# A new table of places and engines for the first recurrence of an attention and MLP kernel

## The chip, the cores and the metric

The kernel runs on one core of a Trainium2 chip. Its time is the device time of one execution in microseconds. A core has a matrix engine (PE, with its weight loads PEld), and the engines DVE, ACT and POOL that work on vectors; SP issues transfers. Matrix results land in PSUM, eight banks of 128 partitions by 512 fp32 numbers, from where DVE or ACT copies them out (an "eviction").

## The reference

The kernel computes a sum of two branches, and the gradients of all inputs for a given gradient of the output:

```
xn  = layernorm(x)                               # x: 2048 x 512
out = x + A(xn) + B(xn)
B:    r = relu(xn @ w1 + b1);  r*r @ w2 + b2     # width 1792
A:    mem = mem0                                 # 8 x 512
      for s in range(64):                        # segments of 32 rows
          h = concat(mem, xn[32*s : 32*s+32])    # 40 rows
          q, k, v = h @ Wq, h @ Wk, h @ Wv       # 32 heads of 128
          p = softmax(mask(q @ k.T / sqrt(128)))
          o = (p @ v) @ Wo                       # 40 x 512
          mem = o[:8];  out_s = o[8:]
```

Branch A is a recurrence: the eight memory rows of a segment come out of the segment before, so 64 segments follow one another, forward and then backward.

## The kernel before

The trace has four stages: the layer norm and the MLP (up to about 227 us), the first recurrence (forward, 227.0 to 1204.5 us), the second (backward), and the gradients of the attention's weights. Only the first recurrence is touched.

**Work of a segment.** The function `chain(s)` (L1535) describes the 32 rows of segment s and what they wait for. On PE it goes: projections of q and k (`proj` L865, matmul L873; two halves each, eight operations of eight matmuls), their transpositions (`to_T` L881, L759), the scores of each half (L1554, L1560), with v's projections beside them; the product of probabilities and values (`bd_half` L976, matmul L983: bd0 and bd1); the product with Wo in four operations (`wo_part` L1434, matmul L1442: wo0 to wo3); and two small matmuls gm0 and gm1 (L1599) that gather the memory rows. Between them: evictions of q, k, v and of the transposes (`evict` L861, copied by DVE in L763 or by ACT in L765), the softmax (DVE L1566 and L1567, ACT L1569, DVE L1573 to L1577), sixteen small copies that spread the probabilities into BDA and BDB (`bd_fill_half` L996, L999, on ACT, DVE or POOL), the normalising eviction of bd's result into oN (DVE L991), two transpositions of oN into OT by DVE (L856), and two half evictions of wo's bank into RFA (L1452). gm0 reads half 0 of RFA and gm1 half 1; DVE copies their results into the next segment's input hA (tile PA, L1603), which its projections wait for: the projections' operations dq 0 for gm0's, dq 1 for gm1's. That closes the chain. A segment also sends seven stores and two copies through SP's queue (L1606 to L1616, issued in L819).

**Blocks and filler.** Four segments make a block, of which there are 16. In each block PE has further work that no segment waits for at once, here called filler: the memory rows that are not in the chain, `l_proj` (L1457, `l_qkv` L1472: projections qL, kL, vL of the next block, evicted into tiles lN0, lN1 and vLN, transposed), and `l_attn` of the previous block (L1488: scores, softmax, product `diag_own` L939, evicted into lN0, stored to S_ONL in L1525, product with Wo); the transposition of hA for the backward pass (`blk_out` L1619, L1628); and in blocks 0 to 13 one `dw_unit` (L1640), a part of the MLP's weight gradients: 32 matmuls (L1655) into two banks, from tiles that SP loads (L1646, L1652), with a transposition of the result (L1669) in blocks 7 to 13. The tile lN0 (in the trace XN) holds first the result of the previous block's `l_attn`, which is stored to S_ONL, and then the next block's qL: the eviction of qL waits for that store.

After the last segment, still in this stage, Wv and Wo are transposed in place for the backward pass: `turn` (L821, called in L1700) in 16 groups of one bank, each with one eviction (tile WA), and `turn_o` (L836, called in L1701) in 16 groups with two evictions each from one bank (tile WB).

**The order.** None of this runs in the order in which it is described. Every operation is given to a plan of the class `_Beat` with the engines that it could run on (`add` L429; `place` L567 gives it a slot). `run` (L573) then takes operations from a heap, smallest place first, once all that they depend on has been taken (`push` L578). The place comes from the table `_FWD` (L28 to L195), three lists of numbers: for the middle blocks 1 to 14 (631 numbers, the same for each), for the first block (493) and for the last (515). In a number x, x//4 is the place in units of 10 ps from the start of the operation's block, a block being `_FWD_BEAT` = 58.393 us long, and x%4 names the engine (0 PE, 1 ACT, 2 DVE, 3 POOL) where an operation has a choice. So the table sets the order on each engine and in each queue, and who does what; the hardware then waits for whatever is not ready. Places in time are the table's own and bind nothing else.

Of the kernel before, what the change touches and what calls it, by code (L numbers as in the profile page):

```python
# [193 lines left out]
    ),  # L194
)  # L195
_FWD_BEAT = 5839300
# [2028 lines left out]
```

## Time and profile before

| what | us |
|---|---|
| median of three runs | 2853.02 |
| the runs | 2841.12, 2853.02, 2857.70 |
| span of the profiled execution | 2847.0 |
| first recurrence in it | 977.5 (227.0 to 1204.5) |
| PE busy in the first recurrence | 934.0 |

The profile is of one more execution. Its span is the time from its first instruction to its last; it lies 6.0 us below the median and between the lowest and the highest run. In lines of the trace, a tile's name stands for the tile that it shares its memory with: XN for lN0 and the other tiles of the memory rows, XK for the transposed keys, PA for hA, P for P40. A bracket at the end of a line is the idle time before it and what ended that.

The blocks of the first recurrence, counted from the first matmul of a block to that of the next, last 58.7, 61.6, 58.5, 59.9, 58.5, 58.2, 58.8, 58.4, 58.3, 59.7, 59.8, 63.6, 58.4 and 56.7 us (blocks 1 to 14).

### The profile page before, as it was taken

Reading aid. Unit: us, or ns where it says so; the run is one execution under the profiler, and the core shown is the slowest. Engines: PE = TensorE matmul, PEld = TensorE weight load, DVE = VectorE, ACT = ScalarE, POOL = GpSimd, SP = SyncE. Lnnn points to the kernel's source line nnn. Section 1 sums busy time; section 2 is a strip of 40 time slices with the busy share of each in tenths; the row PEclk is TensorE's granted clock in tenths of the full one; section 3 lists DMA queues with packets and bytes.
Section 4 is the critical chain, followed back from the end, with each engine's and each line's share of the span. In section 5 each row is a group of like instructions: output and inputs, shape, how many; then the busy total and the mean of one; then the engine's idle time right before and its main releaser. Section 6 shows DMA issues by size and latency. Waiting matters only on the chain.

```text
span 2847.0 us, 114405 instructions
## 1 busy us (share of the span) xinstructions
PE 2708.2 (95%) x47681; PEld 1558.6 (55%) x47681; DVE 1630.3 (57%) x4762; ACT 1191.0 (42%) x2804; POOL 935.3 (33%) x2605
## 2 busy tenths in 40 slices
PE   9999999999999999889998999999999899999999
PEld 7665556566565565655555555555555544444444
DVE  5555666666666567776676666666676502232322
ACT  4334445555555455565554555554554400000000
POOL 1103233223333233344454444444444301111211
PEclk9999999999999999999999999999999999999999
DMA  7648677787777764568898898888888799788861
GB/s 222 208 151 239 190 195 199 211 211 203 208 206 205 194 192 161 147 163 227 224 235 217 219 228 237 221 224 223 227 220 210 224 353 295 229 254 268 254 184 42
DMA packets 556394, 606.28 MB, mean 213 GB/s; under 512 B 228145, under 2 KB 357442, under 8 KB 553826
## 3 DMA queue, kind: packets, MB, share of 16 engines
q1 hardware_dynamic: 540706, 544.88, 70.0%
q0 software_dynamic: 15168, 54.08, 6.1%
q8 instruction: 374, 6.13, 0.9%
q14 instruction: 146, 1.20, 0.1%
HBM read 290.14 MB, written 272.12 MB: 197 GB/s over the span
## 4 chain that ended last, share of the span: by engine, by line
PE 62%; DVE 12%; issue 11%; DMA 7%; ACT 3%; POOL 2%; SPq 2%; DVEq 0%; POOLq 0%; ACTq 0%
PE ps L873 16%; PE ps L2162 10%; PE ps L1777 8%; PE ps L983 5%; PE ps L759 4%; PE ps L1442 4%; PE ps_h L1183 3%; DMA S_GN<-XK 3%; PE ps L1655 3%; PE ps_B L1211 2%; PE ps_gxb L1211 2%; DVE maskA L1963 1%; SPq L819 1%; DVE XN L856 1%; ACT XK L765 1%
## 5 line engine op out<-in xcount | busy, mean ns | idle before, releaser
L873 PE MATMUL ps<-WA,PA 128*32 128x512 bf16 x6144 | 370.8, 380 | 5.3 <-DVE PA L1603 3.8
L2162 PE MATMUL ps<-WA,WB 128*128 128x512 bf16 x1536 | 332.3, 379 | 0.6 <-DVE gwo L763 0.6
L1777 PE MATMUL ps<-WA,XK 128*32 128x512 bf16 x5120 | 315.6, 381 | 9.7 <-DVE XK L856 6.2
L873 PEld LDWEIGHTS <-PA 128*32 128x32 bf16 x8192 | 208.3, 96 | 196.4 <-issue 11.3
L2162 PEld LDWEIGHTS <-WB 128*128 128x128 bf16 x1896 | 185.5, 98 | 224.5 <-issue 0.8
L999 POOL COPY BDA<-PB 32x128 bf16<-32x128 bf16 x468 | 134.9, 288 | 487.3 <-DVE PLp L1571 182.0
L763 DVE CAST gwo<-ps 128x512 bf16<-128x512 f32 x64 | 40.0, 682 | 400.3 <-PE ps L2162 268.3
L765 ACT CAST gwo<-ps 128x512 bf16<-128x512 f32 x64 | 33.1, 599 | 517.2 <-PE ps L2162 357.9
L765 ACT CAST XK<-ps 128x512 bf16<-128x512 f32 x330 | 189.5, 585 | 106.0 <-PE ps L983 61.3
L1777 PEld LDWEIGHTS <-XK 128*32 128x32 bf16 x5120 | 124.6, 97 | 144.9 <-DVE XK L856 36.3
L1777 PE MATMUL ps<-WA,XN 128*32 128x512 bf16 x2560 | 166.1, 385 | 5.9 <-DVE XN L856 5.4
L2173 POOL DMA_DIRECT2D out_dram<-gwo x96 | 71.4, 751 | 295.9 <-ACT gwo L765 264.9
L763 DVE COPY XN<-ps 128x512 bf16<-128x512 bf16 (+1 forms) x146 | 65.7, 450 | 156.5 <-PE ps L759 104.5
L765 ACT CAST XA<-ps 128x512 bf16<-128x512 f32 x141 | 82.8, 587 | 141.7 <-PE ps L873 121.3
L999 ACT COPY BDA<-PB 32x128 bf16<-32x128 bf16 x452 | 133.4, 295 | 14.3 <-DVE PB L1967 2.0
L1442 PE MATMUL ps<-WB,OT 128*32 128x256 bf16 x4096 | 130.7, 275 | 6.7 <-DVE mxA L1577 3.9
L1655 PE MATMUL ps<-XA 128*128 128x512 bf16 x448 | 133.3, 382 | 1.9 <-issue 1.9
L873 PE MATMUL ps<-WB,PA 128*32 128x512 bf16 x2048 | 126.2, 384 | 6.4 <-issue 5.2
L765 ACT COPY XN<-ps 128x256 f32<-128x256 f32 (+2 forms) x158 | 73.9, 480 | 136.5 <-DVE XN L763 75.3
L983 PEld LDWEIGHTS <-XK 128*128 128x128 bf16 x1536 | 94.2, 98 | 61.5 <-POOL XK L999 26.1
L856 DVE STREAM_TRANSPOSE XK<-XK 128x256 f32<-128x256 f32 x256 | 108.7, 436 | 31.8 <-ACT XK L765 28.2
L1005 POOL COPY BDA<-XA 32x256 bf16<-32x256 bf16 x256 | 105.8, 413 | 59.7 <-PE ps L983 34.3
(309 smaller groups left out, 5555.5 us busy)
## 6 DMA issues: line engine op xcount, KB each, us to landing
S_GN<-XK SPq DMA_DIRECT2D x192, 256.0 KB
WA<-S_GN SPq DMA_DIRECT2D x160, 256.0 KB
S_K<-kN SPq DMA_DIRECT2D x64, 256.0 KB
S_Q<-qN SPq DMA_DIRECT2D x64, 256.0 KB
S_V<-vN SPq DMA_DIRECT2D x64, 256.0 KB
S_ON<-oN SPq DMA_DIRECT2D x64, 256.0 KB
XA<-S_Q SPq DMA_DIRECT2D x64, 256.0 KB
XA<-S_K SPq DMA_DIRECT2D x64, 256.0 KB
```

The lines of the kernel that those rows point to most:

```text
L759: nc.tensor.transpose(ps_ap, in_ap, ident[base:base + k, base:base + k])
L765: nc.scalar.copy(out, in_)
L856: self.plan.add({"DVE": 0.36}, lambda e, x=x: nc.vector.transpose(dst[:, x, :, :].rearrange("p i c r -> p (i c r)").bitcast(F32).rearrange ...
L873: nc.tensor.matmul(bk()[32 * j:32 * (j + 1), :], lhsT=win(dc), rhs=Wt(dc, c0), start=(dc == 0), stop=(dc == DC - 1), tile_position=(0, 32 ...
L983: nc.tensor.matmul(bv()[:, n * P:(n + 1) * P], lhsT=B_[:, i, :, :].rearrange("p j k -> p (j k)"), rhs=X[:, i, :], start=(y == 0 and n == 0 ...
L999: self.plan.add({"ACT": 0.31, "DVE": 0.2, "POOL": 0.31}, lambda e, j=j: {"ACT": nc.scalar.copy, "DVE": nc.vector.tensor_copy, "POOL": nc.g ...
L1005: self.plan.add(cost or {"ACT": 0.4, "DVE": 0.27, "POOL": 0.42}, lambda e, j=j: {"ACT": nc.scalar.copy, "DVE": nc.vector.tensor_copy, "POO ...
L1211: nc.tensor.matmul(bk()[:], lhsT=src[z][:, fc, rc * P:(rc + 1) * P], rhs=Wt[:, fc, :], start=(fc == 0 and first), stop=(fc == FC - 1))
L1442: nc.tensor.matmul(bk()[32 * t:32 * (t + 1), :], lhsT=tq(OTt, i, j), rhs=Wo[:, JQ * i + j, h * HB:(h + 1) * HB], start=(i == 0 and j < 2), ...
L1655: A(pe(0.217, "f", 0.11), lambda e, c=c, z=z, x=x: nc.tensor.matmul(bks[x]()[:], lhsT=anT[x][:, c, :], rhs=sx[z][:], start=(c == 0), stop= ...
L1777: nc.tensor.matmul(bk()[32 * j:32 * (j + 1), :], lhsT=tq(XT, i, j), rhs=wtf(t, i, j), start=(first and i == 0), stop=(last and i == NI - 1 ...
L2162: nc.tensor.matmul(bks[n]()[:], lhsT=HNc[:, rc, dc * P:(dc + 1) * P], rhs=half_of(gns[y], hf), start=(y == 0), stop=(y == NRC - 1))
```

## The change

All three lists of `_FWD` are replaced by others of the same lengths. `_FWD_BEAT`, every operation, what it depends on, and all other code stay. Cut to its head, the diff is:

```diff
@@ -27,170 +27,160 @@
 
 _FWD = (
     (
-        -29638520, -28242720, -27012000, -26618480, -60776039, -22458240, -28874400, -22031360, -22336840, -26430039,
...
+        -25597592, -25597580, -25418012, -25178540, -21583191, -21564440, -21564428, -21564416, -21284736, -18683334,
...
 _FWD_BEAT = 5839300
```

What the numbers say, read back into orders and engines:

**Engines.** Of the numbers of a middle block, 99 named ACT, 158 DVE and 60 POOL; now 111, 149 and 57 do. Some 57 operations of a block change their engine, the largest group being 19 from DVE to ACT. All four evictions of q and k are ACT's in the first three segments of a block, and three of four in the last; before they were mixed.

**RFA's two halves (L1452).** Before, ACT took half 1 ahead of DVE's half 0 in segments 1 and 2, and half 0 ahead of DVE's half 1 in segments 3 and 4. Now half 0 is always first, and ACT does both halves in segments 1, 3 and 4; in segment 2 DVE does half 0 and ACT half 1.

**PE's order in a middle block.** The four transpositions of q and k of segments 1 to 3 stand together, q's first in each half; before, one filler (the transposition of `dw_unit`, one of its matmuls, that of `l_proj`) stood between the third and the fourth. The fillers inside a segment stand elsewhere. For the second segment, old and new (dw: a matmul of `dw_unit`; lp: one of `l_proj`; la: one of `l_attn`):

```
old: ... v v v v  4 la  2 dw  bd0  4 dw  bd1  wo0  2 lp  wo1 wo2 wo3  1 lp 2 la  gm0  1 lp 1 la  gm1
new: ... v v v v  4 la  4 dw  bd0  4 dw  bd1  wo0 wo1  2 lp  wo2 wo3  1 lp 2 la  gm0  1 lp 1 la  gm1
```

In the first segment four fillers, `blk_out`'s transposition of the block before among them (before at the end of that block), stand between bd0 and bd1, and two between bd1 and wo0; DVE does the normalising eviction of half 0 behind both sums of the probabilities, a BDB copy and a reciprocal.

**The eviction of qL's first half.** Its place on ACT was ahead of the third segment's k evictions; now it is behind all of that segment's evictions and copies into BDA and BDB. Its transposition on PE was among the third segment's own; now it is behind bd1. The store to S_ONL keeps its place in SP's queue.

**The last block.** PE's part of `l_attn` of block 14 moves from the third segment of block 15 to the second. Of the 16 groups of Wv, eight now come behind the 16 groups of Wo. The evictions of a Wo group are on one engine in 11 of 16 groups (DVE has 21 of the 32, before 19), and DVE has 6 of Wv's 16 (before 7). Behind the last gm DVE has 59 instructions of this stage (before 65) and ACT 40 (before 37).

308 rows, old and new, of the table _FWD are left out of this document.

## The prediction

> **What bounds the kernel now.** I read the page first, then the windows by stage, then PE's waits in steady blocks.
>
> ```profile
> span 2847.0 us, 114405 instructions
> PE 2708.2 (95%) x47681; PEld 1558.6 (55%) x47681; DVE 1630.3 (57%) x4762; ACT 1191.0 (42%) x2804; POOL 935.3 (33%) x2605
> ...
> 227.00:1204.50 977.50, 934.04 (x21105) 577.63 (x21097) 651.51 (x1925) 499.19 (x1171) 301.81 (x828) 0.99 0.72 197
> 1005.30:1063.60 58.30, 57.45 (x1313) 35.37 (x1312) 39.63 (x118) 31.24 (x74) 18.30 (x50) 1.00 0.67 193
> 1063.60:1120.30 56.70, 51.87 (x1283) 32.55 (x1276) 39.86 (x119) 29.60 (x71) 17.77 (x50) 1.00 0.49 159
> ```
>
> The columns of a window are its length, the busy time of PE, PEld, DVE, ACT and POOL, the granted clock, the DMA share and GB/s. The reader is to see that PE is busy 95% of the span, and that only the second window line, the first recurrence, can change: 977.5 us with PE busy for 934.0. So at most 43.5 us of idle PE can be won by a reordering, plus whatever PE loses while busy. Block 13 (the third line) is a good block: 57.45 busy of 58.30. Block 14 has no filler work left, 5.6 us less of it, and is still only 1.6 us shorter. So the chain of dependent steps through four segments is almost as long as the work that fills it, and a steady block has about 1.6 us of slack, 0.4 us per segment. PE's waits in blocks 1 to 13 say where the rest goes.
>
> ```profile
> engine line waited for: us in total, times, longest us
> PE ps L759 <- ACT XN L765: 7.7, 5, 3.4
> PE ps L1442 <- DVE mxA L1577: 3.6, 9, 0.7
> PE ps L873 <- DVE PA L1603: 3.0, 13, 0.2
> PE ps L1599 <- DVE RFA L763: 2.0, 13, 0.2
> ...
> ACT XN L765 <- DMA S_ONL<-XN: 40.5, 9, 8.3
> ...
> DVE RFA L763 <- ACT RFA L765: 58.6, 50, 1.7
> ```
>
> The largest is a transposition (L759) that waits for ACT's eviction of the next block's qL projection. ACT itself waits there, nine times and up to 8.3 us, until a store of lN0 (tile XN) to S_ONL has let go of the tile. The last line is the pair of half evictions of RFA: DVE waits for ACT, which reads the same bank, 50 times.
>
> **The change, part by part.** Nothing is added or removed; orders and engines change.
>
> *A. The eviction behind the store.*
>
> ```profile
> 732.56 0.33 SPq L819 DMA_DIRECT2D S_ONL<-XN  x1
> 736.12 0.58 ACT L765 CAST XN<-ps 128x512 bf16<-128x512 f32 x1 [2.41 <-DMA S_ONL<-XN]
> 744.55 0.29 ACT L999 COPY BDB<-PB 32x128 bf16<-32x128 bf16 x1
> ...
> 384.97 0.58 ACT L765 CAST XN<-ps 128x512 bf16<-128x512 f32 x1 [6.85 <-DMA S_ONL<-XN]
> 385.61 0.61 PE L759 MATMUL ps<-ident,XN 128*128 128x128 bf16 x4 [1.91 <-ACT XN L765]
> 978.18 0.58 ACT L765 CAST XN<-ps 128x512 bf16<-128x512 f32 x1 [8.33 <-DMA S_ONL<-XN]
> ...
> 385.60:389.00 3.40, 3.39 (x65) 1.92 (x69) 1.31 (x4) 2.25 (x5) 0.00 (x0) 0.50 0.26 94
> 979.50:982.90 3.40, 3.40 (x73) 1.70 (x74) 2.10 (x8) 1.85 (x5) 0.33 (x2) 0.50 0.36 121
> ```
>
> In block 8 the store is issued at 732.56 and lets ACT go at 736.12. When the store is late (384.97, 978.18), everything queued behind this eviction on ACT is late: the third segment's k evictions and its transposes, for which PE stands. The new table puts this eviction behind all of the third segment's evictions and fills, that is behind the row at 744.55, 744.84 - 736.12 = 8.7 us later, and moves its transposition from the third segment's own transposes to behind bd1. The store stays where it is in SP's queue, and no other transfer moves past it. The longest wait was 8.3 us, so 8.7 us later the store has landed. Behind the late eviction ACT then has only the RFA half evictions, due 3 us later. That removes PE's 7.7 us.
>
> The two longest of these five waits are each followed by a window at half the clock: PE ran 3.4 us at 0.50, which costs 1.7 us each, 3.4 us together. So A is -7.7 - 3.4 = **-11.1 us**; its bounds are 0 (the store is late by more, or the stall moves to the next thing that waits for it) and -11.1. The Trainium skill (TensorE: Matmul & The Clock Gate, section HAM oscillation) says that the clock is halved only by gaps in PE's work of over about 3.4 us; the trace differs, since the 1.91 us gap before 385.61 was followed by the same half clock. By the page only one of the two stretches would be PE's own doing, and A an estimated 9.4 us.
>
> *B. Steady segments, blocks 1 to 14.* First the half evictions, which gm0, gm1 and the next segment's projections wait for.
>
> ```profile
> 718.88 0.27 ACT L765 COPY RFA<-ps 128x128 f32<-128x128 f32 x1 [3.01 <-PE ps L1442]
> 719.18 0.29 DVE L763 COPY RFA<-ps 128x128 f32<-128x128 f32 x1 [0.89 <-ACT RFA L765]
> 719.52 0.32 PE L1599 MATMUL ps<-selF,RFA 128*32 128x16 f32 x16 [0.16 <-DVE RFA L763]
> ...
> 1134.01 0.49 DVE L763 COPY RFA<-ps 128x128 f32<-128x128 f32 x2 [0.59 <-PE ps L1442]
> ```
>
> The old table has ACT read half 1 first in segments 1 and 2, and DVE half 0, which gm0 needs first, behind it: 718.88 to 719.47 is 0.59 us for both. The new one reads half 0 first everywhere, with ACT doing both in segments 1, 3 and 4 (on one engine, the row at 1134.01, both take 0.49 us). In segment 1 gm0 so gets its half about 0.3 us earlier, while PE idles 2.0/13 + 3.0/13 = 0.38 us per block there. I take all of the 2.0 and half of the 3.0, because hm is still copied by DVE before the projections: -3.5 us, between 0 and -5.0. In segment 2 PE has filler work up to gm0, so an earlier half gains nothing.
>
> Second, in segment 2 two more filler matmuls stand before bd0 and bd1 and the fillers between wo0 and wo1 move behind wo1; wo0's wait for the normalised half (3.6 us, nine times) is covered: -3.6 us, bounds 0 and -3.6.
>
> Third, the transposes of q and k lose the filler that stood among them in segments 1, 2 and 3.
>
> ```profile
> 709.67 0.61 PE L759 MATMUL ps<-ident,qN 128*128 128x128 bf16 x8
> 710.12 0.39 PE L759 MATMUL ps<-ident,XA 128*128 128x128 bf16 x4
> 710.34 0.39 PE L759 MATMUL ps<-ident,kN 128*128 128x128 bf16 x4
> 710.66 0.25 PE L1554 MATMUL ps<-maskA,ident 128*32 128x160 bf16 x4
> ...
> 1124.40 0.61 PE L759 MATMUL ps<-ident,qN 128*128 128x128 bf16 x8
> 1124.97 0.40 PE L759 MATMUL ps<-ident,kN 128*128 128x128 bf16 x4
> 1125.38 0.25 PE L1554 MATMUL ps<-maskA,ident 128*32 128x160 bf16 x4
> ```
>
> With a filler (XA at 710.12) the two q transposes and the last k one follow without a gap: 710.34 - 709.67 = 0.67 us for three groups, and the scores 0.32 us later. Without one (block 15) it is 0.57 us for two groups, 0.12 more than two thirds of 0.67, and 0.41 us to the scores: together 0.2 us in which PE has nothing. The filler's own work is done elsewhere. Segment 1 has such a filler in the 6 blocks with a transposed gradient, segment 2 in 13 blocks, segment 3 in 14: 33 x 0.2 = +6.6 us, between 0 (if the fillers, now elsewhere, cover an equal wait) and +6.6.
>
> Fourth, in segment 1 DVE does oN0 only behind two sums, a fill and a reciprocal; wo's second half of OT comes later. No row shows that order. The nearest is wo's wait above, 0.4 us on average and 0.7 at most: between 0 and 14 x 0.7 = 9.8; I take half the average, because four fillers now stand between bd0 and bd1 and cover part: 14 x 0.2 = +2.8 us.
>
> Fifth, all four q and k evictions go to ACT in segments 1 to 3.
>
> ```profile
> 1122.99 0.59 ACT L765 CAST kN<-ps 128x512 bf16<-128x512 f32 x1 [3.00 <-PE ps L873]
> 1123.48 0.59 ACT L765 CAST qN<-ps 128x512 bf16<-128x512 f32 x1
> ```
>
> ACT takes one every 0.49 us, about as fast as PE finishes them, so I take nothing; if each of the last two waited for the one before it, it would be 0.49 us per segment, which is the rival below. The Trainium skill (TensorEngine Tiling (Array Packing), section PSUM Bottleneck) would have PSUM emptied by ScalarE and VectorE together, against this change; the trace agrees only across banks, since within one bank the two took 0.59 us where one engine took 0.49.
>
> The sum of B is -3.5 - 3.6 + 6.6 + 2.8 = **+2.3 us** (bounds -8.6 and about +19).
>
> *C. The tail.*
>
> ```profile
> 1171.50:1188.50 17.00, 15.83 (x400) 13.44 (x391) 15.01 (x36) 13.08 (x20) 10.82 (x23) 1.00 0.50 123
> 1188.50:1204.50 16.00, 11.57 (x188) 10.28 (x178) 14.99 (x26) 7.22 (x13) 5.87 (x13) 1.00 0.73 180
> ...
> L763 DVE COPY WB<-ps 128x512 bf16<-128x512 bf16 x19 | 11.6, 681 | 0.7 <-ACT WB L765 0.7
> L765 ACT COPY WB<-ps 128x512 bf16<-128x512 bf16 x13 | 7.2, 590 | 9.6 <-DVE WB L763 7.4 <-PE ps L759 2.1
> ```
>
> The last 33 us, where Wv and Wo are turned, are DVE's: busy 30.0 us with 62 instructions, while ACT idles 12.7. ACT's 7.4 us of waiting for DVE are again two readers of one bank. Behind the last gm the new table has six DVE instructions fewer (65 to 59) and three more on ACT. Six of 30.0/62 = 0.48 us are **-2.9 us**, if DVE stays the bound; between 0 and -2.9 - 0.7 (its own waits for ACT).
>
> *D. Blocks 0, 14 and 15.*
>
> ```profile
> 1120.30:1164.40 44.10, 37.79 (x933) 23.86 (x932) 29.58 (x91) 19.27 (x45) 12.75 (x38) 0.96 0.52 170
> ```
>
> In block 15's first three segments PE idles 6.3 us. Block 14's attention of the memory rows moves from the third segment to the second and fills some of it; clock 0.96 of 44.1 says that 1.8 us were lost to a half clock. I take a third of the 6.3, **-2 us**, between -4 and +3 (the third segment then has less to fill). Block 0 is left at nothing.
>
> The sum: -11.1 + 2.3 - 2.9 - 2 = -13.7. The profiled span of 2847.0 becomes 2833.3. It is 6.0 us below the median of the three runs, which stretch over 16.6 us; the forecast is the median's 2853.0 - 13.7 = **2839 us**. A measurement of this kernel can tell about 0.5%, 14.3 us, from no change.
>
> **Rivals.** *R1, the chain becomes the bound (slower).* A steady block has 0.4 us of slack per segment (blocks 13 and 14 above). If each segment's chain waits for one more ACT eviction (0.49), for its second half of RFA on the same engine (0.27), and for the later OT (0.2), it is 0.96 us longer, 0.56 over the slack: 56 x 0.56 = 31 us, less A and C (14.0): +17, **2870 us**. It decides from 14.0/56 = 0.25 us over the slack. For it speaks block 14; against it that the half-0 order shortens the same chain by 0.3 us and that ACT is busy only 31 of 58 us.
>
> *R2, the stall stays.* The store is late because of its queue, not because of ACT; lN0 and its transposition are needed some time, and the eviction now sits in front of the third segment's RFA halves on ACT. Then A is 0: -2.6, **2850 us**. For it: waits of up to 8.3 us against 8.7 of relief leave little. Against: without the two above, the other seven of the nine average (40.5 - 6.85 - 8.33)/7 = 3.6 us.
>
> *R3, all terms at their better ends.* The fillers moved cover as much as they uncovered: -11.1 - 8.6 - 2.9 - 4 = -26.6, **2826 us**. For it speaks that the window has 43.5 us of idle PE; against, that a quarter of that (1.2 + 4.4 + 4.8) lies in the tail and block 14, where the change does little.
>
> **How the numbers follow.** Forecast 0.38 (its own range 2829 to 2849, half of it beyond -14.3 us), R1 0.13, R2 0.27 (2840 to 2858), R3 0.22. Faster by over 0.5%: half the forecast and R3, 0.19 + 0.22 = 0.41. Within: 0.19 + 0.27 = 0.46. Slower: R1, 0.13. The range from 2822 to 2858 holds forecast, R2 and R3 and leaves out R1 and a small part of R3.
>
> **What would show it.** Right: no wait of L759 for ACT XN and no half clock in blocks 1 to 13; DVE's waits for ACT RFA down from 58.6 us to about a quarter; the window of the first recurrence 963 to 965 us; the tail's DVE busy about 27 us. Wrong: PE waiting for qN, kN or qT from ACT (R1), the S_ONL wait on ACT still over 3 us (R2), or wo waiting for OT or mxA in segment 1 by more than 0.4 us a block.

## The result and the profile after

The kernel with the new table is slower: 2862.96 us (median of 11 runs, 2851.32 to 2870.79) against 2845.34 us (11 runs, 2837.14 to 2857.70), a ratio of 1.0062 with a 95% interval from 1.0044 to 1.0080. The forecast was 2839, the range ended at 2858. The base of the forecast was the median of three runs, 2853.0; over eleven runs before is at 2845.3. So the sum was off by 31.3 us (-13.7 forecast, +17.6 measured), more than the two times, 2839 and 2863, suggest.

The profiled execution of after has a span of 2849.5 us; it was the fastest of its 11 runs, 11.6 us under their median, while that of before, a run of about 2849 us, lay some 3.5 us over its own. Line numbers of after are ten smaller than those of before (L1655 is now L1645, and so on); those of the variants further down are the numbers of before. The first fence is after's page, then windows of after: the first recurrence from its first projection (223.8) to the first L1777 matmul of the second recurrence (1227.4), the tail from the last gm on, and two stretches in block 0 and in the tail.

```profile
span 2849.5 us, 114456 instructions
PE 2694.0 (95%) x47537; PEld 1567.1 (55%) x47681; DVE 1553.4 (55%) x4603; ACT 1259.2 (44%) x3007; POOL 920.7 (32%) x2561
...
223.80:1227.40 1003.60, 949.05 (x21395) 603.07 (x21465) 586.87 (x1801) 578.98 (x1389) 291.98 (x796) 0.99 0.72 195
1158.00:1227.40 69.40, 55.33 (x1032) 44.90 (x1033) 42.44 (x89) 34.91 (x55) 20.20 (x48) 0.88 0.44 112
1197.00:1210.60 13.60, 8.92 (x78) 7.98 (x77) 4.99 (x8) 2.94 (x3) 0.00 (x0) 0.51 0.01 1
244.40:254.60 10.20, 5.25 (x64) 2.08 (x67) 0.64 (x3) 0.27 (x1) 0.00 (x0) 0.50 1.26 150
```

The same two stages of before:

```profile
224.50:1221.90 997.40, 953.44 (x21468) 592.78 (x21470) 664.16 (x1960) 510.31 (x1186) 306.35 (x840) 0.99 0.72 196
1164.30:1221.90 57.60, 51.28 (x1044) 41.44 (x1041) 44.31 (x95) 33.42 (x52) 20.70 (x47) 0.97 0.51 133
```

The reader is to see that 6.2 us are lost up to the second recurrence (1003.6 against 997.4), that the tail alone is 11.8 us longer (69.4 against 57.6), and that PE ran at half its clock for 13.6 us on end there, and for 10.2 us in block 0. Of the tail's 11.8 us, PE idles 7.8 more (69.40 - 55.33 against 57.60 - 51.28) and is busy 4.1 more with about as many matmuls, at a mean clock of 0.88 against 0.97. The same difference by blocks, from each block's last gm to the next's: block 0 72.5 against 66.8 us (+5.7); blocks 1 to 14 818.2 against 829.1 (-10.9); block 15's first three segments -0.3; the tail +11.8. So in these two profiles the middle of the stage won about what I had forecast for it (A and B, -8.8), and both of its ends lost more. Whether ordinary executions win it too, the experiments have to say.

PE's waits in blocks 1 to 13 of after, then in block 0, then in the tail:

```profile
PE ps L1645 <- DMA XA<-S_XN: 3.0, 3, 1.7
PE ps L863 <- DVE PA L1593: 2.6, 13, 0.2
PE ps L1645 <- issue: 2.6, 14, 0.6
PE ps L973 <- issue: 1.7, 7, 0.6
PE ps L1645 <- DMA XA<-in_grad_out_dram: 1.4, 2, 1.1
...
PE ps L1432 <- DMA WB<-in_A_Wo_dram: 7.0, 2, 5.9
...
PE ps L749 <- DVE WA L753: 6.3, 7, 2.7
PE ps L749 <- ACT WA L755: 3.5, 5, 1.2
```

And in the tail of before:

```profile
PE ps L759 <- DVE WA L763: 3.3, 3, 2.9
PE ps L759 <- ACT WA L765: 1.0, 4, 0.3
```

Gone are the transpositions' wait for ACT XN (7.7 us before), wo's for mxA (3.6) and gm0's for RFA (2.0). New are waits of `dw_unit`'s matmuls (L1645): 4.4 us for loads of XA and 2.6 us, in 14 pieces, for nothing that the profile names ("issue"); before, they waited once, 1.9 us, for nothing that it names. In block 0 wo3 waits for Wo. In the tail transpositions of WA wait for the evictions of their banks, 9.8 us in all where before had 4.3.

### The profile page after: what moved, and what is told of

Read it like the earlier page. It is cut to its first block, busy times and chain, and to the rows that moved or that the text cites. A ratio compares the mean times of both kernels' runs of the same rounds, so it can differ in the third digit from the quotient of the medians.

```text
span 2849.5 us, 114456 instructions
## 1 busy us (share of the span) xinstructions
PE 2694.0 (95%) x47537; PEld 1567.1 (55%) x47681; DVE 1553.4 (55%) x4603; ACT 1259.2 (44%) x3007; POOL 920.7 (32%) x2561
## 4 chain that ended last, share of the span: by engine, by line
PE 30%; DVE 9%; issue 8%; DMA 8%; ACT 2%; POOL 1%; SPq 1%; DVEq 0%; POOLq 0%; ACTq 0%
PE ps L2152 12%; PE ps L1767 7%; DMA S_GN<-XK 4%; PE ps L863 4%; PE ps L973 3%; PE ps L749 2%; DVE maskA L1953 1%; ACT XK L755 1%; DVE XN L846 1%; DVE XA L1951 1%; DMA WA<-S_GN 1%; PE ps L1982 1%; DVE brA L1950 1%; SPq L809 1%; DVE XA L1948 1%
## 5 line engine op out<-in xcount | busy, mean ns | idle before, releaser
L1767 PE MATMUL ps<-WA,XK 128*32 128x512 bf16 x5120 | 315.8, 381 | 12.8 <-DVE XK L846 6.4
L753 DVE COPY XN<-ps 128x512 bf16<-128x512 bf16 (+1 forms) x167 | 74.1, 444 | 153.6 <-PE ps L749 101.8
L753 DVE COPY XK<-ps 128x512 bf16<-128x512 bf16 x140 | 58.1, 416 | 145.1 <-PE ps L749 98.2
L755 ACT CAST qN<-ps 128x512 bf16<-128x512 f32 x122 | 72.2, 592 | 121.2 <-PE ps L863 107.3
```

Source lines behind the costliest of these rows:

```text
L753: nc.vector.tensor_copy(out, in_)
L755: nc.scalar.copy(out, in_)
L1767: nc.tensor.matmul(bk()[32 * j:32 * (j + 1), :], lhsT=tq(XT, i, j), rhs=wtf(t, i, j), start=(first and i == 0), stop=(last and i == NI - 1 ...
```

## The experiments

Sixteen kernels besides after, each timed beside before on the same chip. Ratios are to before, with 95% intervals. They were timed on several chips, where before's own median lay between 2841.5 and 2848.0 us, so it is the ratios that can be compared from row to row.

| kernel | what it is | median us | ratio |
|---|---|---|---|
| after | | 2862.96 | 1.0062 (1.0044 to 1.0080) |
| x1_mid | before, new middle list | 2894.96 | 1.0175 (1.0144 to 1.0206) |
| x2_first | before, new first list | 2886.22 | 1.0149 (1.0121 to 1.0176) |
| x3_last | before, new last list | 2872.05 | 1.0098 (1.0071 to 1.0125) |
| x4_alt | after, Wv's late groups alternate banks | 2856.80 | 1.0041 (1.0022 to 1.0059) |
| y1_wv_early | after, Wv ahead of Wo | 2857.94 | 1.0044 (1.0027 to 1.0061) |
| y3_both | y1_wv_early, and block 0's loads later | 2849.12 | 1.0015 (0.9998 to 1.0032) |
| z1_oldtail | after, block 0's loads later, tail of before | 2839.45 | 0.9997 (0.9979 to 1.0014) |
| z2_oldtail_ab | z1_oldtail, order of dw's matmuls | 2837.63 | 0.9980 (0.9966 to 0.9995) |
| z3_ab | after, order of dw's matmuls | 2857.46 | 1.0055 (1.0035 to 1.0075) |
| y4_wv_late | before, Wv's groups behind Wo | 2858.11 | 1.0049 (1.0033 to 1.0064) |
| z6_loads_early | before, block 0's loads earlier | 2842.90 | 1.0000 (0.9980 to 1.0020) |
| y5_late_qL | before, qL's eviction later | 2859.17 | 1.0052 (1.0032 to 1.0072) |
| z4_rfa | before, RFA's halves, PE's order not kept | 2846.17 | 1.0015 (0.9993 to 1.0037) |
| z5_rfa_kept | before, RFA's halves, PE's order kept | 2867.76 | 1.0097 (1.0062 to 1.0132) |
| z7_rfa123 | before, RFA's halves in segments 1 to 3 | 2839.99 | 0.9977 (0.9960 to 0.9993) |
| z8_rfa1234 | before, RFA's halves in all four | 2834.25 | 0.9951 (0.9933 to 0.9969) |

The theory after reading the profile: the middle list is faster, and the loss is made at the two ends, by Wo's late load in block 0 and by the place of Wv's groups in the tail. The rival: the middle list is slower in an ordinary execution, and the profiled one, the fastest, hides it.

### One list at a time: x1_mid, x2_first, x3_last

```diff
 _FWD = (middle, first, last)
-(old, old, old)
+(new, old, old)   # x1_mid;  (old, new, old) x2_first;  (old, old, new) x3_last
```

> Only the list for the middle blocks 1 to 14 is the new one; those for the first and the last block are the old ones. Theory 1 (the loss is made at both ends: in block 0, where the weight Wo arrives late, and in the tail, where eight groups of Wv stand behind those of Wo): faster than before by 8 to 12 us, about 2835, since blocks 1 to 14 took 10 us less in the profile of after. Theory 2 (the middle list is slower in an ordinary execution, through waits for the loads of the weight gradients, and the profiled execution of after, its fastest, hides it): slower than before by 5 to 15 us.

> Only the list for the first block is the new one. Theory 1: slower than before by 5 to 10 us, with PE waiting 5 to 7 us for Wo's load in segment 0 and the half clock behind it. Theory 2: the late load was an accident of one execution, and the time is that of before within 3 us.

> Only the list for the last block is the new one, with what follows it: the turns of Wv and Wo. Theory 1: from the last gm to the second recurrence's first L1777 matmul 69 us where before has 58, and slower than before by 6 to 12 us. Theory 2: the second recurrence makes up for its late start, and the time is that of before within 3 us.

Each list alone costs 1.0 to 1.8%, more than the three together, and neither theory expected as much of any of them. The segments' lengths show why: the excess lies at the seams. In x1_mid block 1 took 74.2 us and block 14 73.4, in x2_first blocks 0, 1 and 2 took 80.7, 75.7 and 66.7, in x3_last block 15's first three segments 58.0 against 43.9. A block's fillers belong by number to its neighbours (`l_proj` of the next block, `l_attn` of the last), so one list's places meet another's there. As a test of where the loss is made these three failed; a table of this kind can't be taken apart by lists. Two readings stand: in x2_first Wo came late as in after (see block 0 below), and x3_last's tail took 69.5 us, as expected. Of the middle list they say little: away from the seams, in blocks 2 to 13, x1_mid took 712.8 us, as much as before (713.4) and more than after (701.6), but the profiled execution was the slowest of its six, and z6_loads_early, which has the old middle list, took 703.4 there.

### The tail: x4_alt, y1_wv_early, y4_wv_late

```diff
 after, PE's order behind the last gm (numbers: Wv's groups; o: a group of Wo)
-... 0 1 2 bd 3 bd wo wo wo wo 4 6 dg 5 8 la  16 o  7 9 10 12 14 11 13 15
+... the same                                16 o  7 10 9 12 11 14 13 15             # x4_alt
+... 0 1 2 bd 3 bd 4 5 wo 6 wo wo 7 wo 8 9 dg 10 11 la 12 la 13 la 14 15  16 o       # y1_wv_early
 before
-... 7 6 sc 9 8 wo 11 wo 10 wo wo 13 12 dg 14 15 la  16 o
+... 6 sc 8 wo wo wo wo dg la  16 o  7 9 10 12 14 11 13 15                           # y4_wv_late
```

> After, with one thing changed: the eight groups of Wv behind Wo's come in the order 7, 10, 9, 12, 11, 14, 13, 15 instead of 7, 9, 10, 12, 14, 11, 13, 15, so that consecutive groups use different banks. If a group's wait for the eviction of the same bank makes the tail long, 4 to 6 us less than after there, about 2858. If it is that these groups come late at all (their banks are those of the second recurrence's first turns), less than 2 us.

> After, with the twelve groups of Wv from the fifth on spread among the last segment's steps, in the order of their numbers and all ahead of Wo's groups, as before has them (their evictions on the engines of before). If their place behind Wo makes the tail long: from the last gm to the second recurrence's first L1777 matmul 57 to 60 us instead of 69, and 9 to 12 us faster than after, about 2852. If only the order of banks mattered: as the run with the alternating order, about 2857.

> Before, with eight of Wv's groups (7 and 9 to 15) put behind Wo's groups, in the order and on the engines of after, and nothing else. If that place is what the tail lost: 8 to 12 us slower than before, with 66 to 70 us from the last gm to the second recurrence's first L1777 matmul. If not: within 3 us of before.

The converse is the clearest: in before, the late groups alone cost 0.49% (13.9 us, 9.4 to 18.2, where 8 to 12 were expected), and make the tail 73.6 us long at a clock of 0.86:

```profile
1164.20:1237.80 73.60, 56.82 (x1044) 46.14 (x1046) 46.48 (x97) 31.51 (x50) 20.72 (x47) 0.86 0.41 104
```

How it comes about is read from the timelines of PE and DVE in after, behind Wo's last groups:

```profile
1192.65 0.61 PE L749 MATMUL ps<-ident,WA 128*128 128x128 bf16 x8
1195.95 1.14 PE L749 MATMUL ps<-ident,WA 128*128 128x128 bf16 x16 [2.69 <-DVE WA L753]
1197.87 1.01 PE L749 MATMUL ps<-ident,WA 128*128 128x128 bf16 x8 [0.78 <-DVE WA L753]
1199.67 1.87 PE L749 MATMUL ps<-ident,WA 128*128 128x128 bf16 x16 [0.78 <-DVE WA L753]
1202.70 1.01 PE L749 MATMUL ps<-ident,WA 128*128 128x128 bf16 x8 [1.16 <-ACT WA L755]
1204.81 1.01 PE L749 MATMUL ps<-ident,WA 128*128 128x128 bf16 x8 [1.10 <-ACT WA L755]
...
1185.65 9.65 DVE L753 COPY WB<-ps 128x512 bf16<-128x512 bf16 x16
1195.21 1.28 DVE L753 COPY WA<-ps 128x1024 bf16<-128x1024 bf16 x2
```

The row at 1192.65 is group 7, the next ones are 9 and 10, then 12, then 14 and 11, then 13 and 15. Wv's groups go to two banks by turns, odd numbers to one and even ones to the other, so 9 waits for the eviction of 7 (which DVE does only at 1195.21, after sixteen of Wo's in a row), 12 for that of 10, 14 for that of 12, 13 for that of 11, 15 for that of 13. PE transposes, waits 0.8 to 1.2 us for the eviction, transposes again, with nothing else to do; and a group, 0.61 us long in the first row, takes 1.01 us at half the clock. Alternating the banks took the tail from 69.4 to 65.1 us, as expected; the whole went from 1.0062 to 1.0041, but these intervals overlap. Putting the groups ahead of Wo's gave 62.6 us instead of the expected 57 to 60, and 1.0044: no better than x4_alt within the intervals. The expected 9 to 12 us were not there in that step alone. What was left behind the last gm, the places and engines of Wo's and the other evictions among it, is restored in z1_oldtail.

The gaps that halve the clock are short. The Trainium skill (TensorE: Matmul & The Clock Gate, section HAM oscillation) has the clock fall after idle gaps of over about 3.4 us; here the longest gap of the tail was 2.69 us, and 13.6 us at 0.51 followed it, while shorter gaps kept coming.

### Block 0: y3_both, z6_loads_early

```diff
 SP's queue in block 0 (T: a transposing load L1646, s: a load L1652)
-after:   S_Q S_KL  T T T  s s s s  S_P s S_V T
+y3_both: S_Q S_KL  s s s s s  T T  S_P T S_V T
-before:         S_Q S_KL S_QL  s s s s s  T T  S_KM T S_P S_V T
+z6_loads_early: S_Q S_KL S_QL  T T T  s s s s s  S_KM T S_P S_V
```

> The run with Wv's groups ahead of Wo's, and in block 0 the first three transposing loads of dw_unit's gradients (L1646) put behind the five loads of L1652, as before has them. If these loads hold up Wo's last two: PE's wait for Wo in segment 0 falls from 7 us to 1 to 2, block 0 from 72 us to 66 to 67, and it is 5 to 8 us faster than the run without this change, about 2846: the time of before or a few us less, since blocks 1 to 14 took 10 us less in the profile of after. If Wo's load was late by chance: the time of that run.

> Before, with block 0's first three transposing loads (L1646) ahead of the five loads of L1652, as after has them, and nothing else. If they hold up Wo: PE waits 5 us and more for Wo in segment 0, segment 0 takes 24 us and more instead of 20, and the time is 5 to 9 us above before. If what held Wo up in after was something else: within 3 us of before.

y3_both met its number: 1.0044 to 1.0015, 8.8 us between the two medians; PE's wait for Wo fell to 1.3 us and block 0 to 64.3 us. z6_loads_early missed: no loss at all. The two are reconciled by when the transposing loads start against the last piece of Wo, which POOL issues. SP, POOL and PE of after first:

```profile
233.87 14.78 SPq L1636 DMA_TRANSPOSE XA<-S_AT  x3
...
234.37 0.55 POOL L1391 DMA_DIRECT2D WB<-in_A_Wo_dram  x1
...
248.97 0.62 PE L1432 MATMUL ps<-WB,OT 128*32 128x256 bf16 x8 [5.86 <-DMA WB<-in_A_Wo_dram]
```

and z6_loads_early:

```profile
238.11 8.74 SPq L1646 DMA_TRANSPOSE XA<-S_AT  x3
...
237.51 0.55 POOL L1401 DMA_DIRECT2D WB<-in_A_Wo_dram  x1
...
245.86 0.41 PE L1442 MATMUL ps<-WB,OT 128*32 128x256 bf16 x8 [1.30 <-DMA WB<-in_A_Wo_dram]
```

In after the first transposing load goes out 0.50 us ahead of Wo's last piece, whose reader then starts 14.6 us later; in z6_loads_early 0.60 us behind it, and Wo is on time, though the loads are as early in SP's order. In x4_alt, y1_wv_early and z3_ab, which keep after's order there, they are ahead by 0.50 to 0.51 us, and PE waits 5.1, 6.6 and 7.4 us. x2_first has them ahead by 0.51 us too, and the reader starts 12.8 us after the issue (235.71 to 248.50), though PE, which gets there late, waits only 1.4 us. So the position ahead of the L1652 loads is not the cause by itself. What decides, as far as these traces go, is whether something in SP's queue holds the transposing loads back until Wo is out (the S_QL store in before and z6_loads_early, the L1652 loads in y3_both); no run moved that half microsecond alone.

### Both ends repaired: z1_oldtail

```diff
 after
+block 0's transposing loads as in y3_both
+everything behind the last gm in the order and on the engines of before
```

> After, with block 0's three transposing loads behind the loads of L1652, and with everything behind the last gm in the order and on the engines of before. From the last gm to the second recurrence's first L1777 matmul 57 to 59 us (61 in the run with both repairs), and 2 to 4 us faster than that run, about 2846. If what the tail lost is not in its order, 60 us and more.

The tail took 56.8 us, and the ratio is 0.9997. From after's 1.0062 that is 0.65%, 18.5 us: the two ends account for the whole loss. The tail is 4.1 us shorter than y3_both's 60.9, which is what y1_wv_early had left; in the times the two ratios' intervals overlap.

```profile
1147.40:1204.20 56.80, 50.66 (x1035) 41.16 (x1036) 44.40 (x95) 33.31 (x52) 19.38 (x45) 0.97 0.51 137
```

It also says that the new middle is worth little: in its profile blocks 1 to 14 took 813.8 us against 829.1, but measured it is not faster than before: with both ends repaired the new table is at -0.03% (-0.21 to +0.14), where A and B had -8.8 us, or -0.31%. Three profiles with the old middle list whole and its own neighbours (before, y4_wv_late, z6_loads_early) had 829.1, 828.3 and 818.2 us in these blocks, so single profiles differ by 11 us there. That answers the rival in part: the middle doesn't make the loss, but the gain that after's profile showed in it isn't there in ordinary executions.

### The middle, term A: y5_late_qL

```diff
 before, blocks 1 to 14, third segment
 ACT: -RFA1 | qL k q q |...            +RFA1 | k q q ... BDB | qL | RFA0
 PE:  -q k q qL k ... bd0 bd1 ... wo   +q k q k ... bd0 bd1 qL ... wo | 3 of kL
 the eviction of qL's transposition: ACT -> DVE, as in after
```

> Before, with term A alone: in blocks 1 to 14 the eviction of qL's first half stands behind the third segment's copies into BDA and BDB, its transposition behind bd1, the eviction of that behind OT. kL's first projection, which uses the same bank, moves along, behind wo. If the stall on the S_ONL store was worth what I forecast: no wait of L759 for ACT XN, and 7 to 11 us faster than before. If the moved filler is missed as much ahead of bd0: within 3 us of before.

Slower by 0.52%, where both theories had it no worse than before. The stall is gone, but PE's waits have others in its place (the lines are PE's waits in blocks 1 to 13):

```profile
PE ps L983 <- POOL BDB L999: 6.8, 13, 1.3
PE ps L873 <- DVE XN L763: 6.1, 6, 1.0
PE ps L873 <- ACT XN L765: 4.7, 7, 0.7
```

The third segment went from 14.30 us where nothing stalled it, and 15.33 on average with the stalls, to 15.79 or more in every block: kL's projection needs the bank that qL holds, so three fillers went with it; without them bd0 waits for BDB, and the projections behind wait for the late evictions of XN. A stall that came in five places, 0.6 us per block on average (7.7/13), was exchanged for 1.5 us in every block. This is the move with the other fillers of before left where they are; after has four matmuls of `dw_unit` ahead of bd0 instead, where before and y5_late_qL have one.

### The middle, the loads of dw_unit: z2_oldtail_ab, z3_ab

```diff
-4a 5a 6a 7a 8a 4b 5b 6b 7b 9a 10a 11a 8b 12a 9b 10b 11b 13a 12b 14a 15a 13b 14b 15b
+4a 4b 5a 5b 6a 6b 7a 7b 8a 8b 9a 9b 10a 10b 11a 11b 12a 12b 13a 13b 14a 14b 15a 15b
```

> The run with the tail of before, and besides the matmuls of dw_unit, from the fifth chunk on, in the order 4a 4b 5a 5b 6a 6b and so on, at the places where after has 4a 5a 6a 7a 8a 4b 5b. If PE waits in the second segment because after uses up five loaded chunks there before it gives one back: the waits of L1655 fall from 8 us to under 3 and it is 4 to 7 us faster than the run without this, about 2841, 3 us under before. If the loads are late through the traffic of that time, or if going to and fro between two banks costs PE as much: no faster.

> After, with the matmuls of dw_unit in that order (4a 4b 5a 5b and so on) and nothing else. By the first theory 4 to 7 us faster than after, about 2858, and the steady second segment stays at 14.67 us; by the second no faster.

Not decided by the times: z3_ab's 1.0055 lies in after's interval, z2_oldtail_ab's 0.9980 overlaps z1_oldtail's 0.9997. The theory's number failed, though: waits of L1655 did not fall. z3_ab has 4.6 us of them for loads of XA (after 3.0 + 1.4), and 4.9 us, 31 waits, behind ACT BDB besides.

### The middle, the readers of RFA's bank: z4_rfa, z5_rfa_kept, z7_rfa123, z8_rfa1234

```diff
 before, the two half evictions of RFA in segments 1 | 2 | 3 | 4 (A: ACT, D: DVE, in order)
-A1 D0 | A1 D0 | A0 D1 | A0 D1
+A0 A1 | D0 A1 | A0 A1 | A0 A1          # z8_rfa1234; z7_rfa123 without the last
+ the same, gm0 ahead of two fillers    # z4_rfa
+ the same, an eviction of dw_unit between segment 4's halves   # z5_rfa_kept
```

> Before, with the half evictions of RFA alone as in after (half 0 first; both on ACT in segments 1, 3 and 4, half 0 on DVE and half 1 on ACT in segment 2), in the middle blocks. My forecast for this was 3.5 us faster, at most 5.0: segment 1 shorter by 0.15 to 0.38 us, PE's wait of L1599 for RFA down from 2.0 us. If the waits only move to the copies of hA: no change, within 3 us of before.

> Before, with RFA's half evictions as in after in the middle blocks, and PE's order exactly as before (in the run before, gm0 had moved ahead of two fillers, and PE stood there 12.3 us for ACT). My forecast for this term: segment 1 shorter by 0.15 to 0.38 us, segment 2 the same, 2 to 5 us faster in all. If the old pairs were hidden by the fillers ahead of gm0 already: segments 1 to 4 within 0.1 us of 14.05, 14.99, 14.30, 15.02 and the time within 3 us of before.

> Before, with the new order of RFA's halves in segments 1 to 3 of the middle blocks alone (half 0 first; both on ACT in segments 1 and 3, half 0 on DVE and half 1 on ACT in segment 2), PE's order kept. In the run with all four segments these three were 0.26, 0.30 and 0.16 us shorter than before, and the fourth lost it again, where an eviction of dw_unit stood between ACT's two halves. If that is what the readers of one bank are worth: segments of 13.8, 14.7, 14.15 and 15.0 us, and 6 to 10 us faster than before, about 2836. If other waits take it up: within 3 us of before.

> The same, and in segment 4 too ACT does both halves, one right behind the other. If the fourth segment gains as the others do: 14.8 us or less there, and 2 to 4 us faster than the run with three segments. If in segment 4 gm0 and gm1 stand behind filler anyway: 15.0 us and the same time.

z4_rfa was badly made: gm0 had moved ahead of two fillers, and PE stood there for RFA. z5_rfa_kept too, in segment 4, as ACT shows, where an eviction that waits for a store stands between the halves:

```profile
760.79 0.27 ACT L765 COPY RFA<-ps 128x128 f32<-128x128 f32 x1 [1.72 <-PE ps L1442]
764.40 0.58 ACT L765 CAST XA<-ps 128x512 bf16<-128x512 f32 x1 [3.35 <-DMA out_dram<-XA]
764.88 0.27 ACT L765 COPY RFA<-ps 128x128 f32<-128x128 f32 x1
```

z7_rfa123 and z8_rfa1234 are the clean ones; z7_rfa123 met its numbers, with 14.7 and 14.15 us in the second and third segment and 0.23% (6.6 us). ACT, PE and DVE of z8_rfa1234 at the end of segment 1:

```profile
711.80 0.43 ACT L765 COPY RFA<-ps 128x128 f32<-128x128 f32 x2 [3.01 <-PE ps L1442]
...
711.68 0.61 PE L1655 MATMUL ps<-XA 128*128 128x512 bf16 x2
712.22 0.32 PE L1599 MATMUL ps<-selF,RFA 128*32 128x16 f32 x16
...
712.54 0.27 DVE L1603 CAST PA<-ps 128x16 bf16<-128x16 f32 x2 [1.33 <-PE ps L1599]
```

Both halves are out in 0.43 us instead of 0.59, and gm0 follows the two fillers at once, 0.54 us behind their start instead of 0.76. In segment 2 both tables use both engines, and only the order differs. ACT, DVE and PE there, in block 8 of before, then of z8_rfa1234:

```profile
733.44 0.27 ACT L765 COPY RFA<-ps 128x128 f32<-128x128 f32 x1 [2.70 <-issue]
733.74 0.29 DVE L763 COPY RFA<-ps 128x128 f32<-128x128 f32 x1 [0.85 <-ACT RFA L765]
733.39 0.61 PE L1442 MATMUL ps<-WB,XN 128*32 128x256 bf16 x16
734.09 0.26 PE L1599 MATMUL ps<-selF,RFA 128*32 128x16 f32 x8
...
726.10 0.29 DVE L763 COPY RFA<-ps 128x128 f32<-128x128 f32 x1 [0.51 <-PE ps L1442]
726.46 0.27 ACT L765 COPY RFA<-ps 128x128 f32<-128x128 f32 x1 [3.03 <-issue]
726.09 0.61 PE L1442 MATMUL ps<-WB,XN 128*32 128x256 bf16 x16
726.52 0.22 PE L1599 MATMUL ps<-selF,RFA 128*32 128x16 f32 x8
```

gm0 reads DVE's half in both. Where that half is copied first, gm0 starts 0.43 us behind the start of the filler ahead of it instead of 0.70. The steady segments of the two halves of the stage, that is the length that most blocks have, with nothing stalling them, and those of after for comparison:

| | blocks 1 to 6 | blocks 8 to 13 |
|---|---|---|
| before | 13.81 14.99 14.30 15.05 = 58.15 | 14.05 14.99 14.30 15.02 = 58.36 |
| z8_rfa1234 | 13.80 14.65 14.15 14.89 = 57.49 | 13.98 14.69 14.15 14.86 = 57.68 |
| after | 14.07 14.67 14.39 14.43 = 57.56 | 14.00 14.67 14.39 14.55 = 57.61 |

Segments 2, 3 and 4 gain 0.15 to 0.34 us each, segment 1 up to 0.07: 0.7 us a block, 9 us over thirteen blocks, and 0.49% measured (13.9 us, 8.8 to 19.1). The largest gain, segment 2's, is the order's; in segments 3 and 4 only the engine of the second half changes, and that is worth 0.15 to 0.16 us each. This is the fastest kernel of the study, faster than before and after. And it shows what the rest of the new table is worth in a steady block: nothing, 57.6 against 57.6 us. In ordinary executions the rest even costs: z1_oldtail has the new order of the halves too, and is at 0.9997 where z8_rfa1234 is at 0.9951. Which of the other moves takes this gain back no profile shows.

The Trainium skill's advice to empty PSUM with ScalarE and VectorE together (TensorEngine Tiling (Array Packing), section PSUM Bottleneck) did not pay here for two halves of one bank that are wanted at once: ACT alone took 0.43 us for both where ACT and DVE took 0.59.

## Why the prediction was wrong

The forecast's sum was -13.7 us; measured +17.6. By its steps:

- **C, the tail (-2.9): the step that failed most.** I counted DVE's instructions and took DVE for the bound. DVE's busy time there did fall, from 44.31 to 42.44 us, and the tail got 11.8 us longer all the same: DVE was not its bound. The text before the prediction had eight groups of Wv behind Wo's in its list of changes, and I priced only who evicts them. Their price was their place: alone at the end, two banks by turns, the wait for an eviction between one group and the next of its bank, and the half clock behind the gaps. The tail lost 11.8 us in the profile; putting the groups back ahead of Wo's returned 6.8 of them (y1_wv_early), the rest of before's order there the remainder (z1_oldtail). y4_wv_late, 13.9 us, shows the price of the place by itself.
- **D, block 0 ("left at nothing").** The SP queue's order changed there too, transposing loads ahead of Wo's last piece. I asked of no queue but that of block 8 what else is in flight. The price is 5.7 us in the profile, 8.8 us between the medians of y3_both and y1_wv_early. For block 15 I forecast -2; its first three segments gave -0.3.
- **A (-11.1).** The wait went, as forecast: none of L759 for XN is left in blocks 1 to 13, and the half clock there is gone with it. That it costs nothing was wrong. y5_late_qL shows that this move alone loses 14.8 us; the new table pays for it, as I read it, with its other orders, and with waits of `dw_unit`'s matmuls, 4.4 us for their loads and 2.6 us for nothing that the profile names, where before had 1.9 of the second kind. What is left of A and B together (-8.8) is, by z1_oldtail, -0.03% (-0.21 to +0.14): about -1 us.
- **B (+2.3).** Its upper bound was added up wrongly: 6.6 + 9.8 is 16.4, not about 19. In sum the steady blocks gained: 58.15 to 57.56 and 58.36 to 57.61. RFA's halves were the right mechanism in the wrong size: I took -3.5 us, from segment 1 alone, and said that in segment 2 an earlier half gains nothing since PE has filler up to gm0; segment 1 gave up to 0.07 us a block, and segments 2, 3 and 4 nearly all of the 9 us in z8_rfa1234, segment 2 the most. The wait of wo for mxA went, as forecast. The 0.2 us for each filler missing among the transpositions can't be told from this: against z8_rfa1234, after is longer by 0.24 us in segment 3, which lost one, but not in segment 2, which lost one too, and in segment 1 by 0.27 us in blocks 1 to 6, which lost none, and by 0.02 in blocks 8 to 13, which did. No run tried it by itself. Segment 1's late OT cost next to nothing: wo's wait for OT is 0.6 us in all blocks.
- **The rivals.** The time was R1's sign without R1's mechanism: the chain did not become the bound, steady blocks got shorter. The tail's and block 0's place in the order was no rival of mine, and of the signs that I named for being wrong none appeared: they were all in the middle blocks.
- **What single profiles hide, and what stays open.** Up to the second recurrence, which has the same program, after's profile accounts for only 6.2 of the 17.6 us. Two other profiles show why. z3_ab, which differs from after only in 22 places of `dw_unit`'s matmuls and is timed like it, was profiled in an ordinary run (2861.3 us, mean clock 0.990): its first recurrence takes 1004.5 us, as after's does, with 30.7 us at half clock, all of it in block 0 (10.2), the last block and the tail (20.5), and the rest of its execution has 26.8 us, as before's has (26.3). After's profiled run had only 13.0 us there, so it was lucky behind the first recurrence, not in it. And z6_loads_early, timed like before, takes 988.0 us where before's profile took 997.4; against it after's 1003.6 are 15.6 us longer. That the two ends cause the loss thus rests on z1_oldtail's ratio and on these traces. Open is what in the new table, apart from its ends, takes back what RFA's halves win.

## What to carry to other kernels

When a table or a search moves hundreds of places, price first what comes to stand alone at the end of a queue, and check that consecutive groups there use different PSUM banks. Look at each stage's start for loads that the new order lets out ahead of a load that is needed at once. And here two halves of one bank were read best in the order in which they were wanted (0.30 to 0.34 us in segment 2), by one engine (0.15 to 0.16 us in segments 3 and 4), without anything between them (z5_rfa_kept, segment 4: 15.74 us and more, where before has 15.05). A stage of one trace can be 11 us longer than that of the next with the same program, so compare several before explaining a difference of this size.

## What was not expected of the hardware

Half clock came in stretches of 3.4 us and multiples of it, up to 17.1 us in y4_wv_late. 13.7 us of it followed gaps of 0.8 to 2.7 us in the tail of after. The 10.2 us in block 0 began at 244.5, 1.4 us into the 5.86 us gap (243.11 to 248.97), so the length of a gap doesn't decide it. The 3.4 us ahead of such stretches, one in before and the two longest in after:

```profile
382.20:385.60 3.40, 1.50 (x32) 0.92 (x22) 0.80 (x2) 0.63 (x2) 0.00 (x0) 1.00 0.69 225
...
241.10:244.50 3.40, 0.85 (x24) 0.46 (x17) 0.00 (x0) 0.00 (x0) 0.00 (x0) 0.99 1.07 127
1193.40:1196.80 3.40, 0.85 (x16) 0.85 (x16) 3.09 (x6) 0.08 (x1) 0.00 (x0) 1.00 0.49 160
```

PE was busy for 1.50, 0.85 and 0.85 of 3.40 us. In all eighteen traces, from 20 us on and cut into the 3.41 us steps in which the clock changes, full clock gave way to half only behind a step with PE busy for 1.95 us or less, and always behind one with 1.33 us or less; half clock ended behind every step with more than 3.03 us of busy PE, and behind none with less than 2.52. In after's first recurrence there were 27.3 us at half the clock against 13.7 in before; PE was busy for 17.2 us of them, so they cost at most half of that, 8.6 us, against 6.6 in before.

Three transposing loads that went out half a microsecond ahead of a plain load delayed it: from its issue to the start of its reader 14.6 us (234.37 to 248.97), where it was 8.4 us (237.51 to 245.86) with the transposing loads 0.60 us behind it. In all eighteen traces it was 12.6 to 14.8 us in the five that have them ahead (after, x2_first, x4_alt, y1_wv_early, z3_ab) and 8.1 to 8.9 us in the thirteen that have them behind.
